# Twelve more paired blocks and a new spreading of the FFT, convolution and weight work in a three-stage token-mixing kernel

## The chip, the cores and the metric

The kernel runs on one core of a Trainium2 chip. The metric is the time of one execution on the device in microseconds, the median of the runs. The core has a matrix engine (PE in the profile; its weight loads are PEld), a vector engine (DVE), a scalar engine (ACT), a general engine (POOL) and a queue that only issues transfers (SP). Each of them works through its own list in order; an instruction waits for semaphores that others raise. Matmuls write to PSUM, which has eight banks here; DVE or ACT read ("evict") the result.

## The reference

Inputs are `x` (4 batches, 4224 tokens, 192 channels) and weights. Three functions follow one another:

```python
def _attn_ref(x, weight):            # 8 heads of 24 channels, 7 taps
    w = softmax(weight, axis=-1)
    x_pad = np.concatenate([np.zeros((B, 6, D)), x], axis=1)
    ...
    out = np.einsum('hk,bskhg->bshg', w, x_unf)
def _moe_ref(x, U, V, w_ch1, w_ch2): # U: 4224x32, V: 32x4224, w_ch1: 192x768, w_ch2: 768x192
    h = x.transpose(0, 2, 1) @ U @ V
    u = x + h.transpose(0, 2, 1)
    return u + np.maximum(u @ w_ch1, 0.0) @ w_ch2
def _moe2_ref(x, w_ch1, w_ch2):
    mixed = np.real(np.fft.fft(np.fft.fft(x, axis=1), axis=2))
    u = x + mixed
    un = (u - mean(u)) / np.sqrt(var(u) + 1e-06)
    return u + np.maximum(un @ w_ch1, 0.0) @ w_ch2
```

## The kernel before

**Blocks.** Tokens are handled in blocks of 384 (three tiles of 128). There are 11 blocks per batch and stage, so 88: stage one is `_moe_ref`'s feed-forward part on the convolved tokens, stage two that of `_moe2_ref` after FFT and normalisation. The list `order` sets which batch and stage come when; blocks 0 to 32 are stage one of batches 0 to 2, 33 to 43 stage two of batch 0, 44 to 54 stage one of batch 3, 55 to 87 stage two of batches 1 to 3.

**Two layers.** Numbers are split into a high and a low 16-bit half. `layer1` makes six `unit`s per block (hidden channels in six groups of 128); each accumulates five matmuls of 384 columns in one PSUM bank: four at L663 and one at L653, `last`. Then `evict` writes `hh` on ACT (L648) and, from it and the bank, `hl` on DVE (L649). `layer2` makes three units of 18 matmuls of 192 columns (L696, L698, L700), which read `hh` and `hl` of all six groups; DVE adds the result to the tokens `u` (L706), and SP stores them (`x2d` at L718 after stage one, `out_d` at L722 at the end). In loop step `i` the first layer of block `i` is mixed with the second layer of block `i - 1`.

**Paired blocks.** The second half of the input channels fills 64 rows only. In a block listed in `PAIRED`, `split_high` also makes a copy of it on the other 64 rows (ACT L580, POOL memset L581; 12 transposed pieces instead of 9), so that `last` runs on 64 rows and two neighbours use different halves of the array. All six units come first then, then the six `last`, then the six evictions.

**Preparation.** While block `i` runs, block `i + 2` is prepared: in stage one, adding `h` (L533, L537, or L525 and L528), `sizes` (L543), `scales` (L548, L551), `high` (L555, L578) and `low` (L562); in stage two `stats` (L596, L598), `root` (L603), `normal` (L608 to L617), `high` (L623, L578) and `low` (L629). `low` runs on POOL, or on DVE in the blocks of `LOWV`, and is followed by the transpose `ch<-sp` on SP (L585). `SLOTS` gives each piece its place among twelve in a step.

**Extra work.** The first units are played from the table `START`. The rest stands in `windows`, lists of units that are spread evenly from step `a` to step `z`, three steps per block: loading and decoding the second stage's weights, the convolutions of batches 2 and 3 (`cv` at L399), and for each batch the two halves of the FFT: gathering rows (`xm`, L758), folding them on DVE and POOL (L792 to L797), splitting (L804 to L806), matmuls `s33` (L825), and then `sd`, `s128` and additions (L865 to L915).

The loop over a block's three thirds sets the order on all engines: two units, slots, `play`, one second-layer unit, `fill`.

Of the kernel before, what the change touches and what calls it, by code (L numbers as in the profile page):

```python
# [32 lines left out]
TB = 3  # L33
# [10 lines left out]
SLOTS = [(5, 5, 7, 7, 9, 10), (0, 4, 4, 9, 9)]  # L44
PAIRED = [(5, 11), (22, 34), (76, 88)]
WARM = 52
AGAIN = (18, 44)
# [51 lines left out]
def build(tc, io):  # L99
# [25 lines left out]
    def run(units):  # L125
        for f in units:
            if f is not None:
                f()

    with tc.manual_schedule():  # L130
# [505 lines left out]
        def layer1(s, b, j):  # L636
# [10 lines left out]
            def evict(m):  # L647
                nc.scalar.activation(hh[:, m], acc[m], AF.Relu)  # L648
                nc.vector.scalar_tensor_tensor(out=hl[:, m], in0=acc[m], scalar=0.0,  # L649
                                               in1=hh[:, m], op0=ALU.max, op1=ALU.subtract)  # L650
# [18 lines left out]
            def pairs():  # L669
                for m in range(NM):  # L670
                    last(m, *((slice(64, P), 2, 3) if m % 2 else (slice(0, 64), 1, 1)))
                for m in range(NM):
                    evict(m)

            if kt == 4:
                return [lambda: run([lambda m=m: unit(m) for m in range(NM)] + [pairs])] + \
                    [lambda: None] * (NM - 1)
            return [lambda m=m: unit(m) for m in range(NM)]
# [284 lines left out]
        part(0)  # L963
        load_uv("u", 0, UH)
# [14 lines left out]

        busy(WARM)  # L980

        def over_taps(a):
            return a.unsqueeze(2).broadcast_to([1, H, KW])

        nc.vector.tensor_reduce(out=wmx, in_=wsm, axis=AX.X, op=ALU.max)
        nc.vector.tensor_tensor(out=wsm, in0=wsm, in1=over_taps(wmx), op=ALU.subtract)
        nc.scalar.activation(wsm, wsm, AF.Exp)
        nc.vector.tensor_reduce(out=wmx, in_=wsm, axis=AX.X, op=ALU.add)
        nc.vector.tensor_scalar(out=wmx, in0=wmx, scalar1=1e-9, scalar2=None, op0=ALU.add)
        nc.vector.reciprocal(wmx, wmx)  # L990
        nc.vector.tensor_tensor(out=row[:, :, ::-1], in0=wsm,
                                in1=over_taps(wmx), op=ALU.mult)
        nc.sync.dma_start(rowd[:, nz:KC * H], rowt[:, nz:])

        load_x(0, 0)
        for i in range(2):
            nc.sync.dma_start(tap[KC * i:KC * i + KC].rearrange("p o h -> p (o h)"), bass.AP(
                tensor=rowd.tensor, offset=rowd.offset, ap=[[H, KC], [1, KC * H]]))
# [14 lines left out]
        jobs = dict(v0=lambda: dec_v(0, 2), B0=lambda: busy(AGAIN[0]), B1=lambda: busy(AGAIN[1]), S=lambda: nc.sync.dma_start(sel, io["sel"]),  # L1013
# [8 lines left out]
        def play(t):  # L1022
            for q in START[t].split() if t < len(START) else ():
                if q in jobs:
                    jobs[q]()
                else:
                    if q[0] in "ab" and q[0] not in queues:
                        queues[q[0]] = [f for _, f in ahead("ab".index(q[0]))]
                    for _ in range(int(q[1:] or 1)):
                        f = queues[q[0]].pop(0)  # L1030
                        if f is not None:
                            f()

        START = [
# [7 lines left out]
        windows = [[28, 32, [load_tables]],  # L1042
                   [15, 60, weights_units(1)],
                   [25, 57, [lambda: load_x(2, 0, 0), lambda: load_x(2, 0, 1), None] + conv_units(2)],
                   [37, 70, ft[0][0]], [70, 100, ft[0][1]],
                   [98, 127, ft[1][0]], [125, 153, ft[1][1]],
                   [65, 120, [lambda: load_x(3, 0, 0), lambda: load_x(3, 0, 1), None] + conv_units(3)],
                   [150, 177, ft[2][0]], [179, 197, ft[2][1]],
                   [190, 215, ft[3][0]], [219, 237, ft[3][1]]]
# [9 lines left out]
        last, pre = None, []  # L1059
        for i in range(nblk + 1):  # L1060
            l1 = layer1(*blocks[i]) if i < nblk else [lambda: None] * NM
            pre = [(n - 12, f) for n, f in pre if n >= 12] + ahead(i + 2)

            def at(n):
                run(f for m, f in pre if m == n)

            soon = any(n < nblk and in_pairs(*blocks[n]) for n in (i + 1, i + 2))
            for r in range(TB):
                l1[2 * r]()
                at(4 * r)  # L1070
                l1[2 * r + 1]()
                at(4 * r + 1)
                play(TB * i + r + 1)
                if i == 1:
                    run(last if r == TB - 1 else [])
                elif last:
                    last[r]()
                at(4 * r + 2)
                fill(TB * i + r)
                at(4 * r + 3)  # L1080
            if soon:
                run(f for n, f in pre if n >= 12)
                pre = []
            ahead_load(i + 4)
            last = layer2(*blocks[i]) if i < nblk else None
# [58 lines left out]
```

## Time and profile before

| | |
|---|---|
| median of 3 runs | 993.72 us (991.71 to 994.56) |
| the profiled execution | 1001.54 us, span of its instructions 999.7 us |
| PE busy | 972.6 us, 97% of the span |
| DVE, ACT, POOL busy | 684.3, 593.8, 380.9 us |
| matmuls | 9929 |

PE is busy nearly all the time, so its list of matmuls and its waits decide. A matmul's own duration is longer than its distance to the next one, since they are pipelined; distances between starts, and whole blocks cut out of the timeline, tell what one costs.

### The profile page before, as it was taken

The page shows a single profiled execution, that of the slowest core. Times are in us where ns is not written, and L with a number is a line of the kernel's source. Part 1 is how long each engine was busy: PE and PEld are TensorE (multiplying, and loading weights), DVE is VectorE, ACT ScalarE, POOL GpSimd, SP SyncE. Part 2 cuts the span into 40 slices and gives each one's busy share as a digit, 9 for nine tenths or more (in the row PEclk, how much of TensorE's full clock was granted, in tenths as well). Part 3 has the DMA queues.
Part 4 walks back from the last instruction along what each step waited for, and adds up shares of the span by engine and source line. Part 5 has one row for each costly group of instructions (what it writes and reads, how often), then busy time and mean ns, then how long its engine had stood idle before and what let it go on. Part 6 is the DMA issues. An engine that isn't in the chain of part 4 may idle for free.

```text
span 999.7 us, 25272 instructions
## 1 busy us (share of the span) xinstructions
PE 972.6 (97%) x9929; PEld 761.5 (76%) x9929; DVE 684.3 (68%) x1918; ACT 593.8 (59%) x1336; POOL 380.9 (38%) x398
## 2 busy tenths in 40 slices
PE   8799999999999999999999999999999999999998
PEld 5477767778777787777878888777887887777776
DVE  7775675569775555567776776777777787666663
ACT  2466456655765666657656566666566675556552
POOL 0111011434642334256533545663266751562110
PEclk9999999999999999999999999999999999999999
DMA  8597975755536665354344545432543432542332
GB/s 293 156 251 227 258 180 156 221 169 153 160 98 192 208 200 147 81 140 122 85 111 125 151 139 148 107 93 67 121 114 95 105 98 65 136 110 56 85 84 64
DMA packets 190655, 139.24 MB, mean 139 GB/s; under 512 B 128170, under 2 KB 164113, under 8 KB 189769
## 3 DMA queue, kind: packets, MB, share of 16 engines
q1 hardware_dynamic: 182951, 124.59, 45.8%
q0 software_dynamic: 7104, 12.70, 4.7%
q8 instruction: 77, 1.26, 0.5%
q14 instruction: 41, 0.34, 0.1%
q10 hardware_dynamic: 482, 0.35, 0.1%
HBM read 61.69 MB, written 46.11 MB: 108 GB/s over the span
## 4 chain that ended last, share of the span: by engine, by line
PE 73%; DVE 8%; DMA 7%; issue 5%; POOL 3%; ACT 3%; SPq 0%; DVEq 0%; POOLq 0%; ACTq 0%
PE l L663 27%; PE l L696 11%; PE l L700 10%; PE l L698 10%; PE l L653 6%; PE cv L399 2%; DMA xm<-x2d,mrow 2%; DMA x1d<-xw 2%; PE sd L865 2%; DVE hl L649 2%; PE s L881 2%; POOL xm L758 2%; PE s L825 1%; DVE x L792 1%; DMA ch<-sp 1%
## 5 line engine op out<-in xcount | busy, mean ns | idle before, releaser
L663 PE MATMUL l<-ch,w1h 128*128 128x384 f16 x1584 | 406.3, 327 | 6.7 <-DMA ch<-sp 2.7
L698 PE MATMUL l<-w2l,hh 128*128 128x192 f16 x1584 | 389.5, 246 | 2.4 <-issue 2.3
L700 PE MATMUL l<-w2h,hl 128*128 128x192 f16 x1584 | 389.6, 246 | 1.8 <-DVE hl L649 1.3
L696 PE MATMUL l<-w2h,hh 128*128 128x192 f16 x1584 | 390.1, 246 | 1.1 <-DVE hl L649 0.5
L649 DVE SCALAR_TENSOR_TENSOR hl<-l,hh 128x384 f16<-128x384 f32 x528 | 270.4, 548 | 155.7 <-ACT hh L648 143.0
L648 ACT ACTIVATE hh<-l 128x384 f16<-128x384 f32 x528 | 233.2, 493 | 124.9 <-PE l L653 117.7
L663 PEld LDWEIGHTS <-w1h 128*128 128x128 f16 x1584 | 155.0, 98 | 95.1 <-issue 4.9
L696 PEld LDWEIGHTS <-hh 128*128 128x128 f16 x1584 | 154.7, 98 | 24.1 <-issue 14.0
L663 PE MATMUL l<-ch,w1l 128*128 128x384 f16 x528 | 172.3, 326 | 0.4 <-issue 0.4
L698 PEld LDWEIGHTS <-hh 128*128 128x128 f16 x1584 | 155.0, 98 | 11.0 <-issue 1.8
L700 PEld LDWEIGHTS <-hl 128*128 128x128 f16 x1584 | 154.9, 98 | 4.3 <-DVE hl L649 2.3
L562 POOL TENSOR_TENSOR sp<-un,sp 128x576 f16<-128x576 f32 x44 | 57.4, 1306 | 249.7 <-ACT sp L578 207.3
L653 PE MATMUL l<-ch,w1l 128*128 128x384 f16 (+1 forms) x528 | 133.7, 327 | 0.0
L758 POOL DMA_INDIRECT xm<-x2d,mrow x84 | 84.6, 1007 | 21.3 <-issue 18.1
L629 POOL TENSOR_TENSOR sp<-un,sp 128x576 f16<-128x576 f32 x34 | 44.1, 1296 | 116.8 <-ACT sp L578 107.2
L623 ACT ACTIVATE un<-u,mr,rs 128x192 f32<-128x192 f32 x132 | 62.4, 537 | 19.6 <-DVE mr L617 19.0
L663 PEld LDWEIGHTS <-w1l 128*128 128x128 f16 x528 | 51.8, 98 | 28.6 <-issue 4.9
L851 POOL DMA_INDIRECT u<-x2d,mrow x64 | 62.2, 972 | 15.3 <-issue 11.4
L653 PEld LDWEIGHTS <-w1l 128*128 128x128 f16 (+1 forms) x528 | 40.4, 97 | 34.2 <-issue 9.9
L578 ACT ACTIVATE sp<-un 128x576 f16<-128x576 f32 x88 | 60.1, 683 | 3.1 <-DMA ch<-sp 0.4
L543 ACT ACTIVATE junk<-u 128x576 f16<-128x576 f32 x44 | 30.0, 681 | 44.2 <-issue 20.0
L706 DVE SCALAR_TENSOR_TENSOR u<-l,ws,u 128x384 f32<-128x384 f32 x88 | 44.2, 510 | 13.8 <-PE l L700 7.8
(137 smaller groups left out, 1135.8 us busy)
## 6 DMA issues: line engine op xcount, KB each, us to landing
x2d<-u SPq DMA_DIRECT2D x68, 288.0 KB
u<-x1d SPq DMA_DIRECT2D x44, 288.0 KB
out_d<-u SPq DMA_DIRECT2D x43, 288.0 KB
x1d<-xw SPq DMA_DIRECT2D x36, 210.0 KB
u<-x2d SPq DMA_DIRECT2D x32, 192.0 KB
x<-x2d SPq DMA_DIRECT2D x60, 99.0 KB
xw<-x_d SPq DMA_DIRECT2D x4, 1344.0 KB
xw<-x_d SPq DMA_DIRECT2D x8, 672.0 KB
```

What stands on the lines that cost most here:

```text
L562: low_engine(0, b, j).tensor_tensor(out=sp[:, :, D:2 * D], in0=k["un"], in1=sp[:, :, :D], op=ALU.subtract)
L578: nc.scalar.activation(sp[:, :, :D], k["un"], AF.Identity)
L623: nc.scalar.activation(un[:, t], u[:, t], AF.Identity, scale=k["r"][:, t:t + 1], bias=k["m"][:, t:t + 1])
L648: nc.scalar.activation(hh[:, m], acc[m], AF.Relu)
L649: nc.vector.scalar_tensor_tensor(out=hl[:, m], in0=acc[m], scalar=0.0, in1=hh[:, m], op0=ALU.max, op1=ALU.subtract)
L653: nc.tensor.matmul(acc[m].rearrange("p (r n) -> p r n", r=TB), lhsT=w["l1"][rows, n, m * P:(m + 1) * P], rhs=kd[x][rows], start=False, sto ...
L663: nc.tensor.matmul(o, lhsT=w[v][:, e, ms], rhs=kd[x], start=(n == 0), stop=False)
L696: nc.tensor.matmul(o, lhsT=hh[:, m, rs], rhs=w["h2"][:, m], start=(m == 0), stop=False)
L698: nc.tensor.matmul(o, lhsT=hh[:, m, rs], rhs=w["l2"][:, m], start=False, stop=False)
L700: nc.tensor.matmul(o, lhsT=hl[:, m, rs], rhs=w["h2"][:, m], start=False, stop=(m == NM - 1))
L758: nc.gpsimd.indirect_dma_start(out=xs[c][1][:, g], out_offset=None, in_=x2d[b][:], in_offset=bass.IndirectOffsetOnAxis(ap=mrow[:99, k:k + ...
L851: nc.gpsimd.indirect_dma_start(out=u2[:, s0 + 2 * e], out_offset=None, in_=src[:], in_offset=bass.IndirectOffsetOnAxis(ap=mrow[:, k2 + e - ...
```

## The change

Forty-two blocks are paired instead of thirty: 4, 11, 12, 20, 21, 34 and 70 to 75 are new. The loop body is replaced by two strings, one for unpaired and one for paired blocks, in which `u` is a unit of the first layer, `l` one of the second layer of the block before, `e` an eviction of a paired block, `a` the next slot of preparation, `p` a step of `START`, `f` a step of the windows. The six evictions of a paired block stand in two groups, five (with a slot between the third and fourth) and one. `SLOTS` and `windows` have other numbers, and the first jobs, before the loop, are named in `START` in the order in which they stood.

```diff
-SLOTS = [(5, 5, 7, 7, 9, 10), (0, 4, 4, 9, 9)]
-PAIRED = [(5, 11), (22, 34), (76, 88)]
+SLOTS = [(3, 4, 7, 7, 9, 10), (0, 4, 4, 9, 10)]
+SEQ = ["uualapfaauauaplafauauaplafa", "uuuauuueeeaeeplafpaaalaeaafaplafa"]
+PAIRED = [(4, 13), (20, 35), (70, 88)]
...
             def pairs():
                 for m in range(NM):
                     last(m, *((slice(64, P), 2, 3) if m % 2 else (slice(0, 64), 1, 1)))
-                for m in range(NM):
-                    evict(m)
-
+
+            units = [lambda m=m: unit(m) for m in range(NM)]
             if kt == 4:
-                return [lambda: run([lambda m=m: unit(m) for m in range(NM)] + [pairs])] + \
-                    [lambda: None] * (NM - 1)
-            return [lambda m=m: unit(m) for m in range(NM)]
+                units[-1] = lambda: (unit(NM - 1), pairs())
+                return units, [lambda m=m: evict(m) for m in range(NM)]
+            return units, []
...
-        windows = [[28, 32, [load_tables]],
-                   [15, 60, weights_units(1)],
-                   [25, 57, [lambda: load_x(2, 0, 0), lambda: load_x(2, 0, 1), None] + conv_units(2)],
+        windows = [[31, 34, [load_tables]],
+                   [9, 58, weights_units(1)],
+                   [28, 57, [lambda: load_x(2, 0, 0), lambda: load_x(2, 0, 1), None] + conv_units(2)],
                    [37, 70, ft[0][0]], [70, 100, ft[0][1]],
-                   [98, 127, ft[1][0]], [125, 153, ft[1][1]],
-                   [65, 120, [lambda: load_x(3, 0, 0), lambda: load_x(3, 0, 1), None] + conv_units(3)],
-                   [150, 177, ft[2][0]], [179, 197, ft[2][1]],
-                   [190, 215, ft[3][0]], [219, 237, ft[3][1]]]
+                   [98, 127, ft[1][0]], [129, 157, ft[1][1]],
+                   [62, 130, [lambda: load_x(3, 0, 0), lambda: load_x(3, 0, 1), None] + conv_units(3)],
+                   [144, 177, ft[2][0]], [179, 197, ft[2][1]],
+                   [190, 215, ft[3][0]], [219, 239, ft[3][1]]]
...
-            for r in range(TB):
-                l1[2 * r]()
-                at(4 * r)
-                l1[2 * r + 1]()
-                at(4 * r + 1)
-                play(TB * i + r + 1)
...
-                at(4 * r + 2)
-                fill(TB * i + r)
-                at(4 * r + 3)
+            for q in SEQ[bool(evicts)]:
+                if q == "u" and l1:
+                    l1.pop(0)()
+                elif q == "e":
+                    evicts.pop(0)()
+                elif q == "l" and last:
+                    last.pop(0)()
+                elif q == "a":
+                    run(f for m, f in pre if m == slot)
+                    slot += 1
...
```

**On PE, in block 20.** Before, the second layer of block 19 follows on the second unit of block 20 (`l1_4093` and `l1_4101` are the banks of units 0 and 1, `l2_4110` that of the second layer):

```order
L663 MATMUL l1_4101<-ch_3901,w1h0_92 128x384
L653 LDWEIGHTS w1l0_93
L653 MATMUL l1_4101<-ch_3901,w1l0_93 128x384
L696 LDWEIGHTS hh_3927
L696 MATMUL l2_4110<-w2h0_94,hh_3927 128x192
```

Now it follows on the six paired matmuls of all six units; line numbers of the changed kernel are one or two lower (`l1_4118`, `l1_4123` and `l1_4128` are the banks of units 3 to 5):

```order
L652 MATMUL l1_4118<-ch_3912,w1l0_93 128x384
L652 LDWEIGHTS w1l0_93
L652 MATMUL l1_4123<-ch_3912,w1l0_93 128x384
L652 LDWEIGHTS w1l0_93
L652 MATMUL l1_4128<-ch_3912,w1l0_93 128x384
L694 LDWEIGHTS hh_3937
L694 MATMUL l2_4150<-w2h0_94,hh_3937 128x192
```

So the second layer of block 19, which needs the evictions of block 19, moved back by four units.

**On DVE, in block 81, near the end, where no extra work stands.** Before, the evictions of block 81 (`l1_14602` and `l1_14607` are its units 4 and 5) come first, and the statistics for block 83 after them:

```order
L649 SCALAR_TENSOR_TENSOR hl_14581<-l1_14602,hh_14580 128x384
L649 SCALAR_TENSOR_TENSOR hl_14581<-l1_14607,hh_14580 128x384
L596 BN_STATS st_14630<-u2_13258 128x6 x3
L598 BN_AGGR mv_14631<-st_14630 128x2 x3
L608 RECIPROCAL rs_14659<-sd_14657 128x3
```

Now the statistics come first, then the evictions of units 0 to 4:

```order
L595 BN_STATS st_14621<-u2_13310 128x6 x3
L597 BN_AGGR mv_14622<-st_14621 128x2 x3
L648 SCALAR_TENSOR_TENSOR hl_14605<-l1_14606,hh_14604 128x384
L648 SCALAR_TENSOR_TENSOR hl_14605<-l1_14611,hh_14604 128x384
L648 SCALAR_TENSOR_TENSOR hl_14605<-l1_14616,hh_14604 128x384
L648 SCALAR_TENSOR_TENSOR hl_14605<-l1_14629,hh_14604 128x384
L648 SCALAR_TENSOR_TENSOR hl_14605<-l1_14634,hh_14604 128x384
L607 RECIPROCAL rs_14681<-sd_14679 128x3
```

The statistics moved in front of the evictions, and the eviction of unit 5 moved behind `normal` and the addition of a second-layer result (L704 in the changed kernel).

## Rows read from the trace of the kernel before

**Rows 1.** The page: busy time, share of the span and instructions of each engine.
```profile
PE 972.6 (97%) x9929; PEld 761.5 (76%) x9929; DVE 684.3 (68%) x1918; ACT 593.8 (59%) x1336; POOL 380.9 (38%) x398
```

**Rows 2.** PE's waits: for whom, us in total, times, longest.
```profile
PE l L663 <- DMA ch<-sp: 2.7, 2, 2.2
PE l L663 <- DVE hl L649: 2.5, 1, 2.5
PE s L825 <- POOL xp L806: 2.3, 3, 1.4
...
PE am L122 <- DVE gm L337: 1.1, 1, 1.1
```

**Rows 3.** Timeline, block 20: start, us, engine, line, instruction, [idle before].
```profile
275.35 0.33 PE L663 MATMUL l<-ch,w1h 128*128 128x384 f16 x1
...
276.19 1.19 DVE L792 TENSOR_TENSOR x<-x,xm 99x760 f32<-99x760 f32 x1 [1.92 <-DMA xm<-x2d,mrow]
...
279.32 0.26 PE L700 MATMUL l<-w2h,hl 128*128 128x192 f16 x1 [1.03 <-DVE hl L649]
```

**Rows 4.** Timeline, block 9, DVE and PE.
```profile
153.19 0.25 DVE L173 TENSOR_SCALAR dec<-u 128x192 int32<-128x192 int32 x1
...
155.12 1.01 DVE L649 SCALAR_TENSOR_TENSOR hl<-l,hh 128x384 f16<-128x384 f32 x2
...
155.72 0.24 PE L533 MATMUL h<-gst,vst 96*128 96x192 f16 x1 [1.76 <-DVE hl L649]
```

**Rows 5.** Timeline of PE, end of block 56.
```profile
675.95 0.67 PE L825 MATMUL s<-vt,xp 99*97 99x102 f16 x10 [1.43 <-POOL xp L806]
```

**Rows 6.** Windows of blocks 70, 72, 80, 81: length, busy us, clock, DMA share, GB/s.
```profile
core 0: us, PE busy (x) PEld busy (x) DVE busy (x) ACT busy (x) POOL busy (x), PEclk, DMA share, GB/s
...
815.01:825.15 10.14, 10.14 (x106) 8.19 (x104) 9.97 (x29) 7.78 (x18) 3.10 (x3) 1.00 0.24 61
834.74:844.07 9.33, 9.33 (x87) 7.39 (x85) 6.39 (x20) 5.01 (x13) 0.00 (x0) 1.00 0.25 65
919.00:928.06 9.06, 9.06 (x87) 6.94 (x86) 5.55 (x19) 5.07 (x13) 1.58 (x3) 1.00 0.31 76
928.06:937.11 9.05, 9.05 (x86) 6.93 (x85) 5.55 (x19) 5.05 (x13) 1.53 (x2) 1.00 0.32 79
```

**Rows 7.** Timeline of PE, end of the first layer of paired block 28.
```profile
366.73 0.49 PE L663 MATMUL l<-ch,w1h 128*128 128x384 f16 x2
367.15 0.66 PE L653 MATMUL l<-ch,w1l 64*128 64x384 f16 x6
367.74 0.26 PE L696 MATMUL l<-w2h,hh 128*128 128x192 f16 x1
```

**Rows 8.** Groups by line and shape: count, busy us, mean ns, idle before.
```profile
L653 PE MATMUL l<-ch,w1l 128*128 128x384 f16 x348 | 113.8, 327 | 0.0
...
L653 PE MATMUL l<-ch,w1l 64*128 64x384 f16 x180 | 19.8, 326 | 0.0
...
L580 ACT ACTIVATE sp<-un 128x192 f16<-128x192 f32 x30 | 10.4, 346 | 0.0
```

**Rows 9.** Timeline of the tail, SP, POOL and PE; block 82 starts at 937.11.
```profile
932.85 1.38 SPq L585 DMA_TRANSPOSE ch<-sp  x1
...
934.33 0.87 SPq L722 DMA_DIRECT2D out_d<-u  x1
...
936.63 0.26 POOL L581 MEMSET sp<- 128x192 f16 x1 [3.81 <-DMA ch<-sp]
...
937.11 0.33 PE L663 MATMUL l<-ch,w1h 128*128 128x384 f16 x1
```

**Rows 10.** Two windows of 4 us, columns as in rows 6.
```profile
82.00:86.00 4.00, 4.00 (x46) 2.98 (x45) 3.11 (x10) 3.26 (x7) 0.89 (x1) 1.00 0.04 15
...
102.00:106.00 4.00, 3.95 (x58) 2.96 (x60) 3.21 (x7) 3.09 (x8) 0.00 (x0) 1.00 1.09 143
```

**Rows 11.** Timeline, SP and PE; block 38 starts at 474.92.
```profile
470.18 1.26 SPq L585 DMA_TRANSPOSE ch<-sp  x1
...
474.92 0.33 PE L663 MATMUL l<-ch,w1h 128*128 128x384 f16 x1
```

More of the change, by code (lines that the diff above doesn't have):

```diff
@@ L42 @@
 PIECE = 5
-SLOTS = [(5, 5, 7, 7, 9, 10), (0, 4, 4, 9, 9)]
-PAIRED = [(5, 11), (22, 34), (76, 88)]
-WARM = 52
-AGAIN = (18, 44)
+SLOTS = [(3, 4, 7, 7, 9, 10), (0, 4, 4, 9, 10)]
+SEQ = ["uualapfaauauaplafauauaplafa", "uuuauuueeeaeeplafpaaalaeaafaplafa"]
+PAIRED = [(4, 13), (20, 35), (70, 88)]
 W_MIN, W_MAX = (float(np.array(w, np.uint32).view(np.float32)) for w in (0x38000000, 0x47EFFFFF))
@@ L962, in build @@
         part = w0_st["st"]["part"]
-        part(0)
-        load_uv("u", 0, UH)
         zer = wrk.tile([1, KC * H], F32, name="hl", tag="hl")
@@ L978, in busy, with soft, taps @@
                                  start=True, stop=True)
-        busy(WARM)
         def over_taps(a):
             return a.unsqueeze(2).broadcast_to([1, H, KW])
[L985 to L998, printed above, removed]
+        def soft():
+            nc.vector.tensor_reduce(out=wmx, in_=wsm, axis=AX.X, op=ALU.max)
+            nc.vector.tensor_tensor(out=wsm, in0=wsm, in1=over_taps(wmx), op=ALU.subtract)
+            nc.scalar.activation(wsm, wsm, AF.Exp)
+            nc.vector.tensor_reduce(out=wmx, in_=wsm, axis=AX.X, op=ALU.add)
+            nc.vector.tensor_scalar(out=wmx, in0=wmx, scalar1=1e-9, scalar2=None, op0=ALU.add)
+            nc.vector.reciprocal(wmx, wmx)
+            nc.vector.tensor_tensor(out=row[:, :, ::-1], in0=wsm,
+                                    in1=over_taps(wmx), op=ALU.mult)
+            nc.sync.dma_start(rowd[:, nz:KC * H], rowt[:, nz:])
+        def taps():
+            for i in range(2):
+                nc.sync.dma_start(tap[KC * i:KC * i + KC].rearrange("p o h -> p (o h)"), bass.AP(
+                    tensor=rowd.tensor, offset=rowd.offset, ap=[[H, KC], [1, KC * H]]))
         uf = ut.rearrange("p n r -> p (n r)")
@@ L1012, in build @@
                       z=[lambda n=n: dec_v(n, n + 1) for n in range(2, 6)])
-        jobs = dict(v0=lambda: dec_v(0, 2), B0=lambda: busy(AGAIN[0]), B1=lambda: busy(AGAIN[1]), S=lambda: nc.sync.dma_start(sel, io["sel"]),
+        jobs = dict(v0=lambda: dec_v(0, 2), M=soft, T=taps, U0=lambda: load_uv("u", 0, UH), S=lambda: nc.sync.dma_start(sel, io["sel"]),
                     V=lambda: load_uv("v", 0, TB * P), V12=lambda: load_uv("v", TB * P, 3 * TB * P),
@@ L1025, in play @@
                     jobs[q]()
+                elif q[0] == "B":
+                    busy(int(q[1:]))
                 else:
@@ L1057, in fill @@
                     done[n] = upto
-        last, pre = None, []
+        last, pre = [], []
         for i in range(nblk + 1):
-            l1 = layer1(*blocks[i]) if i < nblk else [lambda: None] * NM
+            l1, evicts = layer1(*blocks[i]) if i < nblk else ([], [])
             pre = [(n - 12, f) for n, f in pre if n >= 12] + ahead(i + 2)
-            def at(n):
-                run(f for m, f in pre if m == n)
             soon = any(n < nblk and in_pairs(*blocks[n]) for n in (i + 1, i + 2))
-            for r in range(TB):
-                l1[2 * r]()
-                at(4 * r)
-                l1[2 * r + 1]()
-                at(4 * r + 1)
-                play(TB * i + r + 1)
[L1074 to L1077, printed above, removed]
-                at(4 * r + 2)
-                fill(TB * i + r)
-                at(4 * r + 3)
+            slot = steps = fills = 0
+            if i == 1:
+                last = [lambda: None] * 2 + [lambda q=last: run(q)]
+            for q in SEQ[bool(evicts)]:
[8 more added lines that the diff above has]
+                    slot += 1
+                elif q == "p":
+                    play(TB * i + steps + 1)
+                    steps += 1
+                elif q == "f":
+                    fill(TB * i + fills)
+                    fills += 1
             if soon:
@@ L1084, in build @@
             ahead_load(i + 4)
-            last = layer2(*blocks[i]) if i < nblk else None
+            last = layer2(*blocks[i]) if i < nblk else []
         assert all(d == len(w[2]) for d, w in zip(done, windows))
```

2 rows, old and new, of the table START are left out of this document.

## The prediction

> **What bounds the kernel now.** I read the page first. PE is busy for 972.6 of the 999.7 us span, DVE for 684.3, ACT for 593.8, POOL for 380.9 [rows 1], so the end is set by PE's queue, and a change is worth what it takes from PE's matmuls or from the places where PE stands. The list of PE's waits comes next: the longest entries are only 2.7, 2.5, 2.3 and 1.1 us in total [rows 2]. The 2.5 and most of the 2.7 (a single wait of 2.2) fall in front of and inside block 0, where the change alters little. The timeline, cut at the first L663 matmul of each block, shows three of the later ones. In block 20 (first matmul at 275.35) PE had done units 0 and 1 and was inside the second layer of block 19; it stood 1.03 us for `hl` of block 19, because on DVE that eviction stood behind L792, which had itself waited 1.92 us for gathered rows [rows 3]. In block 9 PE stood 1.76 us in L533, for a PSUM bank that `hl` had to free; DVE had first decoded a piece of weights from 153.19 to 155.12 [rows 4]. At the end of block 56 PE stood 1.43 us for POOL's L806, a step of the FFT work [rows 5]. So PE's long waits after block 0 come to 2.3 (all L825) + 1.76 + 1.03 + 1.1 (an `am` matmul, for DVE) = 6.2 us.
>
> How long a block is without extra work is seen where no window has units: block 72, unpaired, is 9.33 us; blocks 80 and 81, paired, are 9.06 and 9.05, PE busy from end to end in all three [rows 6].
>
> **The change, part by part.**
>
> *Twelve more paired blocks* (4, 11, 12, 20, 21, 34, 70 to 75). A paired block runs its six last first-layer matmuls on 64 rows each, two at a time. It is 9.33 - 9.055 = 0.28 us shorter [rows 6]. The joint of a paired block says where the rest of the halving goes: the last two full-height matmuls take 0.42 us from start to start (366.73 to 367.15) and the six half-height ones 0.59 (367.15 to 367.74) [rows 7]. A full-height one costs 9.33 / 57 = 0.164 us (30 of 384 columns and 54 of half that), so the eight would take 1.31 and take 1.01: 0.30, the same saving. That is in line with the busy times of the two forms, 113.8 us for 348 full-height and 19.8 for 180 half-height ones, though a single one lasts as long (327 and 326 ns) [rows 8]. I take 0.28: 12 x 0.28 = **-3.4 us**. The Trainium skill, TensorEngine Tiling (Array Packing), Theoretical Speedup, gives up to twofold for two row tiles; by that the six would cost three slots and the saving would be an estimated 0.49 each, 5.9 us in all, and the sum below would end at 985.5. The same page, Key Properties, says that changing the tiling mode drains the array, and the longer joint above agrees with that.
>
> What pairing adds does not lie on PE: one more ACT copy of 346 ns (L580) per block [rows 8], a POOL memset, and a transpose of twelve pieces rather than nine. ACT is idle for 40% of the span [rows 1]; if that cover were gone, twelve copies would cost 12 x 0.35 = 4.2 us.
>
> *Cover for late evictions.* The PE rows of block 20 show the second move. In an unpaired block the second layer of the block before follows after two units, ten matmuls or 1.6 us; in a paired one after all six, 24 x 0.164 + 0.59 = 4.5 us. The 1.03 us wait [rows 3] is shorter than the 2.9 us that this adds, so it goes: **-1.0 us**. What is late next: the same `hl` is needed 2.9 us later, and behind it DVE has five evictions whose users come a whole block later.
>
> *Two groups of evictions, preparation in front.* In a paired block DVE used to do six evictions and then the statistics for the block after next. Now statistics (or, in stage one, nothing) come first, five evictions, then preparation, then the sixth behind one L706. PE needs the sixth only in the next block's second layer, over 4 us later, so I cost it at nothing; if it were the limit, a late sixth eviction costs one L649 (0.55 us) per paired block at most, 23 us over 42. What it buys is slack: in the tail the transpose for block 82 starts at 932.85, POOL sees it land at 936.63 and PE starts on it at 937.11, 0.5 us to spare [rows 9]. No time is lost there now, so nothing is gained either.
>
> *Weights of stage two loaded and decoded earlier* (window from step 9 rather than 15). The load of 2.3 MB moves from about 105 us, where the DMA engines are full (share 1.09), to about 78 us, ahead of a stretch with a share of 0.04 [rows 10]; decoding then is over before block 9, whose 1.93 us between 153.19 and 155.12 stood in front of its evictions [rows 4]. The ACT eviction before them was itself late, so I take a third: **-0.6 us** (bounds 0 and -1.76).
>
> *FFT windows.* The first half of batch 2 gets steps 144 to 177 instead of 150 to 177, 33 steps for the same 17 units; its `s33` matmuls, twice per block in blocks 53 to 57, come three times in two blocks. That should end the waits for L806 there: of the 2.3 us of L825 I take **-1.5** (bounds 0 and -2.3). The other windows move work between blocks in which PE is full before and after: nothing.
>
> *What twelve more paired blocks can add in waits.* Paired blocks hold six PSUM banks until their evictions; block 9's wait is of this kind, the one long one in 30. Spread over 12 blocks: 1.76 x 12 / 30 = **+0.7** (bounds 0 and, with one like it in every second block, +10).
>
> *Start and end.* The starting part has the same rows on every engine up to block 0, and the last block is paired in both: nothing.
>
> Sum: -3.4 - 1.0 - 0.6 - 1.5 + 0.7 = -5.8 us. The profiled execution took 1001.5 us (span 999.7 and 1.8 around it), 7.8 above the median of 993.7; the terms are differences within PE's queue, so I take them off the median: 987.9, say **988**.
>
> **Rivals.**
>
> *A. Only the matmuls shrink* (chance 0.22). The waits change place and keep their sum: 993.7 - 3.4 = 990.3. For it: nothing removes L792's wait for its gathered rows, it is only hidden. Against: the waits of blocks 20 and 56 [rows 3, 5] stand in blocks whose order changes in the right direction.
>
> *B. Nearly all waits go* (0.15): -3.4 and the whole 6.2 us: 984.1.
>
> *C. The evictions become the bound* (0.14). PE's part of a paired block shrinks, DVE's does not. In block 70, now paired, DVE is busy for 9.97 of 10.14 us [rows 6]; with 0.28 taken off PE it lacks 0.11. If the twelve blocks all were so, none would shorten, and the waits would be no fewer: about 993.5. Against it: in block 72 DVE has 6.39 of 9.33. The Trainium skill, TensorEngine Tiling (Array Packing), PSUM Bottleneck, warns of this: tiling speeds up TensorE but not the emptying of PSUM. By that rule none of the pairing would show.
>
> *D. Slower: the transpose comes too late in stage two* (0.07). Slot 9 became 10 for `low`, so it and its transpose now stand behind the third second-layer unit: 18 short matmuls, 9 x 0.164 = 1.5 us, and on SP behind the `out_d` store, whose issue takes 0.87 us [rows 9]: up to 2.3 us later. In block 38 the transpose started at 470.18 for a use at 474.92, 4.74 us [rows 11]; one takes at most 936.63 - 932.85 = 3.8 [rows 9]. The spare is 0.9, so such a block would lose 1.4 us. It decides from five such blocks among stage two's unpaired ones (with the 5.8 gained); with six it ends near 996, with seven near 998. Against it: in block 38 POOL was late for other reasons, which hold the slot's place anyway, and in the paired tail the statistics start 3 us earlier than the transpose is put back.
>
> **How the numbers follow.** Forecast 0.42 (985 to 990.5), A 0.22, B 0.15, C 0.14, D 0.07. No change means within 0.3%, 990.7 to 996.7, about what a measurement of this kernel can tell. Faster: the forecast, B, and half of A, whose 990.3 lies at the bound: 0.68. Same: the other half of A, C, and a third of D: 0.27. Slower: 0.05. The range goes from 983, 1 us under B, to 993.5, C's time, and leaves out D and the tails of B and C, under 0.2. A and C end on the side of no gain, so the likeliest case has its own range, 985 to 990.5.
>
> **What would show it.** In the profile after: PE busy down by 3 to 4 us and the half-height L653 matmuls 252 instead of 180; blocks 72 to 75 shorter by 0.28 for the same extra work; no wait of PE for `hl` in the second layer in block 20; none for L806 in blocks 53 to 57; in the tail 1 us or more between the landing of the transpose and its use. I am wrong if PE's waits for `ch` add up to more than 3 us (D), if DVE is full over several paired blocks and PE waits for `hl` there (C), or if the weights' load at 78 us delays a `ch` or `u` of blocks 4 to 6.

## The result and the profile after

The changed kernel takes 983.48 us (median of 5 runs, 983.06 to 984.84) against 992.34 us of the kernel before in the same comparison (5 runs, 991.71 to 994.56): ratio 0.9909, interval 0.9896 to 0.9922. It is 8.9 us faster. The forecast was 5.8 us (988). The stated range, 983 to 993.5, just holds the time; the range of the likeliest case, 985 to 990.5, does not; and rival B (984.1) was nearer than the forecast.

The page of the profiled execution after (span 981.3 us), beside [rows 1]:

```profile
PE 964.2 (98%) x9929; PEld 755.6 (77%) x9929; DVE 688.2 (70%) x1918; ACT 595.7 (61%) x1348; POOL 388.4 (40%) x410
```

The same 9929 matmuls keep PE busy for 8.4 us less. About 3 us of that belong to the one execution that was profiled before: in a second profile of that kernel (before_look, below) the same 9162 matmuls from block 4 on keep PE busy for 893.8 us instead of 896.9. PE's longest waits after, beside [rows 2] (for whom, us in total, times, longest; line numbers are one or two lower than before):

```profile
PE l L662 <- DVE rc L550: 2.2, 1, 2.2
PE l L662 <- DVE hl L648: 1.8, 1, 1.8
...
PE am L121 <- DVE gm L336: 1.1, 1, 1.1
...
PE s L823 <- POOL xp L804: 1.0, 2, 0.5
...
PE s L823 <- DVE z L831: 0.7, 1, 0.7
```

The first two stand in front of and inside block 0, as before. The waits for `xp` fell from 2.3 to 1.0 (what is left stands in blocks 19 and 20), those for `hl` in the second layer and in L533 (now L532) have left the list, and one for DVE's `z` is new, in block 19. The timeline after, beside [rows 3, 4]: first block 9 (DVE and PE), then block 20 (PE):

```profile
151.47 2.42 DVE L648 SCALAR_TENSOR_TENSOR hl<-l,hh 128x384 f16<-128x384 f32 x5 [1.42 <-ACT hh L647]
...
152.66 0.41 PE L532 MATMUL h<-gst,vst 96*128 96x192 f16 x3
...
273.48 0.32 PE L662 MATMUL l<-ch,w1h 128*128 128x384 f16 x1 [0.34 <-DVE cmax L547]
...
274.91 0.66 PE L652 MATMUL l<-ch,w1l 64*128 64x384 f16 x6
275.50 0.26 PE L694 MATMUL l<-w2h,hh 128*128 128x192 f16 x1
...
281.53 0.67 PE L823 MATMUL s<-vt,xp 99*97 99x102 f16 x10 [0.50 <-POOL xp L804]
```

In block 9 the evictions run without a decoding in front of them and PE does not stand in L532. In block 20 the second layer (from 275.50) runs without a wait for `hl`, but PE now waits inside the units for `cmax`, and for `xp` at the block's end. Windows of blocks 70, 72 and 80 after, columns as in [rows 6]:

```profile
800.44:810.31 9.87, 9.87 (x106) 7.75 (x104) 9.61 (x28) 7.15 (x18) 3.29 (x4) 1.00 0.29 71
819.62:828.67 9.05, 9.05 (x86) 6.93 (x85) 6.82 (x22) 5.53 (x14) 0.26 (x1) 1.00 0.32 78
...
901.02:910.08 9.06, 9.06 (x88) 6.94 (x85) 6.98 (x23) 5.54 (x14) 1.53 (x2) 1.00 0.32 78
```

Blocks 70 and 72, newly paired, are 0.27 and 0.28 us shorter (10.14 to 9.87 and 9.33 to 9.05). Block 70 did so with DVE at 9.61 of 9.87 us. The groups of the last first-layer matmul, beside [rows 8], and the tail, beside [rows 9], where block 82 now starts at 919.13:

```profile
L652 PE MATMUL l<-ch,w1l 128*128 128x384 f16 x276 | 90.0, 326 | 0.0
L652 PE MATMUL l<-ch,w1l 64*128 64x384 f16 x252 | 27.8, 326 | 0.0
```

```profile
912.95 1.45 SPq L584 DMA_TRANSPOSE ch<-sp  x1
...
916.72 0.26 POOL L580 MEMSET sp<- 128x192 f16 x1 [3.79 <-DMA ch<-sp]
```

The transpose has landed 2.4 us before its use; before, it was 0.5.

### The profile page after: what moved, and what is told of

It reads as the page before. It is cut to its first block, busy times and chain, and to the rows that moved or that the text cites. A ratio compares the mean times of both kernels' runs of the same rounds, so it can differ in the third digit from the quotient of the medians.

```text
span 981.3 us, 25290 instructions
## 1 busy us (share of the span) xinstructions
PE 964.2 (98%) x9929; PEld 755.6 (77%) x9929; DVE 688.2 (70%) x1918; ACT 595.7 (61%) x1348; POOL 388.4 (40%) x410
## 4 chain that ended last, share of the span: by engine, by line
PE 90%; DMA 4%; DVE 2%; ACT 1%; issue 1%; POOL 1%; SPq 0%; ACTq 0%; DVEq 0%; POOLq 0%
PE l L662 34%; PE l L694 13%; PE l L698 13%; PE l L696 13%; PE l L652 7%; PE s L823 2%; PE cv L398 2%; PE sd L863 2%; PE s L879 2%; DMA x1d<-xw 1%; PE gp L414 1%; PE h L532 1%; DMA u<-wc_d 1%; DMA ch<-sp 1%; DMA tap<-rowd 1%
## 5 line engine op out<-in xcount | busy, mean ns | idle before, releaser
L662 PE MATMUL l<-ch,w1h 128*128 128x384 f16 x1584 | 395.4, 326 | 5.2 <-DVE rc L550 2.2
L698 PE MATMUL l<-w2h,hl 128*128 128x192 f16 x1584 | 389.6, 246 | 0.0
L698 PEld LDWEIGHTS <-hl 128*128 128x128 f16 x1584 | 154.9, 98 | 1.2 <-issue 1.1
L561 POOL TENSOR_TENSOR sp<-un,sp 128x576 f16<-128x576 f32 x44 | 59.3, 1348 | 203.8 <-ACT sp L577 174.2
L652 PE MATMUL l<-ch,w1l 128*128 128x384 f16 (+1 forms) x528 | 117.8, 326 | 0.0
L628 POOL TENSOR_TENSOR sp<-un,sp 128x576 f16<-128x576 f32 x34 | 45.2, 1330 | 84.6 <-ACT sp L577 80.9
L652 PEld LDWEIGHTS <-w1l 128*128 128x128 f16 (+1 forms) x528 | 35.8, 96 | 33.9 <-issue 13.3
L704 DVE SCALAR_TENSOR_TENSOR u<-l,cmax,u 128x384 f32<-128x384 f32 x88 | 44.9, 511 | 14.2 <-PE l L698 13.6
```

The lines of the kernel that those rows point to most:

```text
L561: low_engine(0, b, j).tensor_tensor(out=sp[:, :, D:2 * D], in0=k["un"], in1=sp[:, :, :D], op=ALU.subtract)
L652: nc.tensor.matmul(acc[m].rearrange("p (r n) -> p r n", r=TB), lhsT=w["l1"][rows, n, m * P:(m + 1) * P], rhs=kd[x][rows], start=False, sto ...
L662: nc.tensor.matmul(o, lhsT=w[v][:, e, ms], rhs=kd[x], start=(n == 0), stop=False)
L698: nc.tensor.matmul(o, lhsT=hl[:, m, rs], rhs=w["h2"][:, m], start=False, stop=(m == NM - 1))
```

## The experiments

All kernels are the changed one with constants put back or varied. Three parts can be exchanged: the list of pairs (P), the order inside a block (O: the two strings and `SLOTS`), and the windows (W). The old order, written as strings:

```diff
-SLOTS = [(3, 4, 7, 7, 9, 10), (0, 4, 4, 9, 10)]
-SEQ = ["uualapfaauauaplafauauaplafa", "uuuauuueeeaeeplafpaaalaeaafaplafa"]
+SLOTS = [(5, 5, 7, 7, 9, 10), (0, 4, 4, 9, 9)]
+SEQ = ["uauaplafauauaplafauauaplafa", "uuuuuueeeeeeaaplafaaaplafaaaplafa"]
```

The runs of one group below shared one chip, each group another, and every ratio is against the kernel before on that chip.

| group | kernel | P O W | median us | ratio, interval |
|---|---|---|---|---|
| 1 | before | | 1002.37 | |
| 1 | pairs_only | new old old | 1003.9 | 1.0015, 0.9999 to 1.0032 |
| 1 | order_only | old new old | 1001.63 | 0.9997, 0.998 to 1.0014 |
| 1 | windows_only | old old new | 998.8 | 0.9966, 0.9949 to 0.9982 |
| 2 | before | | 993.05 | |
| 2 | after_again | new new new | 983.31 | 0.991, 0.9883 to 0.9937 |
| 2 | no_pairs | old new new | 987.16 | 0.9944, 0.9927 to 0.9961 |
| 2 | no_order | new old new | 987.88 | 0.9943, 0.9923 to 0.9963 |
| 2 | no_windows | new new old | 990.47 | 0.9981, 0.9962 to 1.0 |
| 3 | before | | 1001.68 | |
| 3 | weights_late | new new, weights old | 996.84 | 0.9945, 0.9928 to 0.9961 |
| 3 | fft_old | new new, FFT old | 997.72 | 0.9961, 0.9944 to 0.9977 |
| 3 | windows_only_2 | old old new | 999.1 | 0.9977, 0.9961 to 0.9992 |
| 3 | pairs_only_2 | new old old | 1003.27 | 1.002, 1.0003 to 1.0038 |
| 4 | before | | 994.06 | |
| 4 | whole_third | new new new | 983.82 | 0.9896, 0.9874 to 0.9917 |
| 4 | pairs_only_3 | new old old | 991.84 | 0.9977, 0.9961 to 0.9993 |
| 4 | prep_behind | one string other | 987.88 | 0.9932, 0.9908 to 0.9955 |
| 4 | all_paired | 84 pairs | 991.24 | 0.9978, 0.9961 to 0.9995 |
| 5 | before | | 994.16 | |
| 5 | thirteen_more | 55 pairs | 979.41 | 0.9855, 0.9829 to 0.9881 |

**Each part alone** (group 1). Theory 1: the parts add up, as the terms of the prediction do. Theory 2, its rival: pairing pays only with the new order. With it the kernel before was profiled once more, for PE's waits without a releaser ("issue" in the list of waits: time in which PE waited for nothing that the profile shows). In the first profile of before they came to 5.5 us from block 4 on.

> Only the list of paired blocks is new (42); order within a block, slots and windows as before. Theory 1, the parts add up: PE's matmuls shrink by 12 x 0.28 = 3.4 us and the waits of PE stay, so 989 us beside 992.3 for the kernel before, with block 72 at 9.05 us. Theory 2, pairing pays only with the new order of evictions and preparation: in the twelve new blocks PE waits take back 2 us or more, 991 us or above.

> Only the order within a block and the slots are new (evictions in two groups, preparation in front); 30 paired blocks, windows as before. Theory 1: PE's waits inside the old paired blocks (6, 8, 9, 26, 76, 86, together 4.7 us in the profile before) shrink by 1 to 3 us, the others stay: 989.5 to 991.5. Theory 2: the order has no gain of its own, 992 +-1, since it only makes room for more pairs.

> Only the windows of extra work are new. Theory 1: the waits of blocks 53 to 56 for the FFT's splitting go (2.8 us) and so does the 1.9 us in block 9, behind the decoding of weights: 988 us, 4 us less than before. Theory 2: the windows only fit the shorter blocks; waits move elsewhere, 991 to 993.

> The kernel before, profiled a second time. Its first profile spans 999.7 us though its runs have a median of 992.3, and holds about 7.6 us in which PE waits for nothing that the profile shows (blocks 14, 33, 42, 64, 73). Theory 1: these belong to that one execution; the second profile lacks them and spans about 991 us, with the same waits for hl, xp and gm at the same blocks. Theory 2: they belong to the kernel, and stand at the same blocks again.

On this chip only the windows gave something measurable. The second profile of before took 1005.34 us and showed the waits without a releaser again. Theory 1 had expected 3.4 us less for the pairs; that fell. In order_only the wait that rival D described does stand in one place, in front of block 38:

```profile
473.00 0.34 PE L662 MATMUL l<-ch,w1h 128*128 128x384 f16 x1 [1.29 <-DMA ch<-sp]
```

On SP the transpose now follows the `out_d` store, as D said. No profile of before has this wait; so the order by itself made one there. But the chip was another one, so the whole change had to be measured beside its parts.

**One part left out** (group 2).

> The whole change, on the same chip as the runs with one part left out. Additive theory: the three parts alone gave 1.0015 (pairs), 0.9997 (order) and 0.9966 (windows) of the kernel before, so that together they give 0.998. Interaction theory: the 0.991 of the first measurement comes back, and 0.7% of it belongs to parts only in company. If it is 0.991, the three runs beside it, each with one part taken out, say which company.

> Order and windows new, the 30 old paired blocks. If pairing pays its 0.28 us a block once the new order is there, this stands 3 to 4 us above the whole change (0.9945 of before). If the pairs bring nothing even then (as pairs alone did), it stands within 1 us of it (0.991 to 0.992). Additive theory: 0.9963.

> 42 paired blocks and new windows, with the old order inside a block (six units, six evictions, preparation behind them). If the new order is what makes pairs pay, 12 more pairs here bring nothing over windows alone: 0.996 to 0.998 of before, 5 to 7 us above the whole change. If windows are what makes pairs pay, 0.992 to 0.993. Additive theory: 0.998.

> 42 paired blocks and the new order, old windows. If the new order makes pairs pay, 0.9955 to 0.9965 of before (3.4 us of matmul time, less than the whole change by the windows' 3.4 us). If only the windows make pairs pay, 1.000 as the order alone and the pairs alone. Additive theory: 1.001.

The whole change keeps its 0.991. Leaving out the pairs costs 3.9 us, the order 4.6, the windows 7.2. These sum to 15.6, more than the 9.7 of the whole (993.05 - 983.31): each part's worth includes waits that only the other parts make or leave room for. The profiles from block 4 on say the same: 3.0, 3.2 and 6.2 us more than after_again. In no_windows PE stands for `hl` again in block 9 (1.58) and for `xp` in blocks 55 and 56 (0.60 and 1.43), but also in block 6 (1.1; 0.5 in the first profile of before, none in the later before_look) and in front of block 38 (0.53, for `ch`; none in any profile of before). So with the old windows the new order and pairs make waits of their own. With windows and pairs together (no_order) the ratio is lower than with windows alone in group 1, but that is another chip; whether pairs pay with the old order is shown by pairs_only_3 below. In the profile of no_pairs, block 20 (unpaired there) has its old wait back:

```profile
274.29 0.26 PE L698 MATMUL l<-w2h,hl 128*128 128x192 f16 x1 [0.87 <-DVE hl L648]
```

Yet that block takes 11.96 us in no_pairs and 11.66 after: 0.30, the pairing's own 0.28 and nothing for the cover.

**Two windows put back, two parts alone again** (group 3).

```diff
-                   [9, 58, weights_units(1)],
+                   [15, 60, weights_units(1)],
```

> The whole change with only the weights' window put back to start at step 15. Theory W: the decoding in front of block 9's evictions was worth the whole of its wait: 1.8 to 2.0 us above the whole change (0.993 of before), with the wait of about 1.75 us of L533 (or what stands there) back in block 9 or next to it. The prediction's term: 0.6 us above. If early weights matter in more places (the transfers of the weights against the transposes of blocks 1 to 6), more than 2.5 us.

```diff
-                   [98, 127, ft[1][0]], [129, 157, ft[1][1]],
+                   [98, 127, ft[1][0]], [125, 153, ft[1][1]],
...
-                   [144, 177, ft[2][0]], [179, 197, ft[2][1]],
-                   [190, 215, ft[3][0]], [219, 239, ft[3][1]]]
+                   [150, 177, ft[2][0]], [179, 197, ft[2][1]],
+                   [190, 215, ft[3][0]], [219, 237, ft[3][1]]]
```

> The whole change with only the three FFT windows put back (second halves of batches 1 and 3, first half of batch 2). Theory F: the waits of the s matmuls for POOL's xp in blocks 53 to 57 come back, 2.3 to 2.8 us above the whole change (0.9935 of before). The prediction's term: 1.5 us above. If the windows' worth of 7 us in company lies mostly here: 4 us or more.

> The windows alone once more, where the PE time without a releaser (7 us in the profiles of before, pairs alone, order alone and windows alone, none in the whole change and in the three kernels with one part left out) may be absent. Theory chip: this idle time belongs to the chip or the execution; where it is absent the windows alone give 5 to 7 us (0.993 to 0.995) and the parts add up nearly. Theory company: windows alone give 0.9966 again.

> The twelve further pairs alone once more. Theory chip: 0.9965 (3.4 us of matmuls less). Theory company: 1.000 to 1.002 again, with the data waits of PE in blocks 20, 33, 34, 55, 73 and 76 that took the saving the first time.

weights_late: the decoding is back in front of block 9's evictions, and PE stands in L532 again:

```profile
153.24 0.25 DVE L172 TENSOR_SCALAR dec<-u 128x192 int32<-128x192 int32 x1
...
155.18 2.41 DVE L648 SCALAR_TENSOR_TENSOR hl<-l,hh 128x384 f16<-128x384 f32 x5
...
155.78 0.24 PE L532 MATMUL h<-gst,vst 96*128 96x192 f16 x1 [1.59 <-DVE hl L648]
```

A second wait, 0.75 us for DVE's L122, stands in block 6 at 114.52. fft_old: the waits for `xp` in blocks 53 to 57 are back, the longest of them as before [rows 5], and in block 73 PE stands for `rp`:

```profile
673.83 0.57 PE L823 MATMUL s<-vt,xp 99*97 99x102 f16 x8 [1.43 <-POOL xp L804]
...
850.21 0.20 PE L879 MATMUL s<-rp,vt 128*128 128x97 f16 x1 [1.22 <-ACT rp L868]
```

The whole change was not run on this chip. Against its 0.99 elsewhere, the two ratios put the weights' window at about 4 us and the FFT windows at 5 to 6 us. PE's data waits that are back, and that the whole change does not have, come to 2.7 us in blocks 6 and 9 for the weights, and to 4.4 us for the FFT, 2.6 of them in blocks 53 to 56 and the rest in blocks 73 and 76. The parts alone gave here about what they gave in group 1.

**The pairs alone on a chip like that of group 2, the order's core, and all pairs** (group 4).

> The whole change on whichever chip this is. If the gain belongs to the kernel: 0.991 of before again, also where PE's waits without a releaser are there. If it came only where those are absent, and a chip that has them takes part of it: 0.994 to 0.997.

> The twelve further pairs alone. On a chip with PE's waits without a releaser: 1.002 again. On a chip without them: 0.9965 if only those waits ate the saving; 1.000 if the data waits in blocks 73 and 76 and the late transposes of the tail do.

```diff
-"uuuauuueeeaeeplafpaaalaeaafaplafa"
+"uuuuuueeeeeeaaplafpaaalaaafaplafa"
```

> The whole change with the string of a paired block changed alone: six units, six evictions, then the preparation. The prediction's price for two groups and preparation in front: nothing, so within 1 us of the whole change. If this is what the new order is worth: 3 to 5 us above it, with waits for ch or sd in blocks 82 to 86 and for rp in block 73, as the kernel with the old order showed.

```diff
-PAIRED = [(4, 13), (20, 35), (70, 88)]
+PAIRED = [(4, 88)]
```

> Blocks 4 to 87 all paired, 42 more than in the whole change. If the term of 0.28 us holds in every block: 11.8 us less than the whole change. If late second layers and held banks cost where DVE, ACT and POOL carry FFT work (rival C): less than half of it, or slower, with PE waiting for hl or u in blocks 13 to 19 and 35 to 69.

pairs_only_3 gains 2.2 us of the 3.4; in groups 1 and 3 the same kernel gained nothing. So pairs can pay with the old order, and theory 2 in its strict form falls as well. They also make waits. before_look and pairs_only_3, both without the waits that lack a releaser, differ by the twelve pairs alone; PE at the same place in block 73, first without and then with them:

```profile
843.02 0.43 PE L881 MATMUL s<-rp,vt 128*128 128x97 f16 x6
```

```profile
844.92 0.38 PE L879 MATMUL s<-rp,vt 128*128 128x97 f16 x5 [1.02 <-DVE rp L869]
```

From block 4 on, PE is busy for 2.9 us less in pairs_only_3 and idle for 2.6 us more. prep_behind is 4.1 us slower than the whole change (medians of six runs each, with ranges that do not overlap). Its profile shows one place clearly, block 73 (DVE and PE):

```profile
838.06 1.01 DVE L648 SCALAR_TENSOR_TENSOR hl<-l,hh 128x384 f16<-128x384 f32 x2
...
838.99 0.87 DVE L595 BATCH_NORM_STATS2 st<-u 128x6 f32<-128x192 f32 x3
...
841.84 0.35 DVE L869 TENSOR_TENSOR rp<-sd,rp 128x194 f16<-128x194 f32 x1
...
842.24 0.38 PE L879 MATMUL s<-rp,vt 128*128 128x97 f16 x5 [1.36 <-DVE rp L869]
```

Statistics and their small followers stand between the evictions and the product of the FFT (L869) that PE needs. After the whole change the statistics are done before the evictions, and L869 comes in time:

```profile
829.21 0.87 DVE L595 BATCH_NORM_STATS2 st<-u 128x6 f32<-128x192 f32 x3
...
837.75 0.35 DVE L869 TENSOR_TENSOR rp<-sd,rp 128x194 f16<-128x194 f32 x1
838.00 0.54 PE L879 MATMUL s<-rp,vt 128*128 128x97 f16 x6
```

all_paired is 7.4 us slower than the whole change, although 42 blocks more are paired. PE's waits there:

```profile
PE l L662 <- DMA ch<-sp: 9.6, 6, 2.2
PE s L823 <- POOL xp L804: 4.5, 7, 1.2
PE s L823 <- DVE z L831: 2.4, 3, 1.7
```

They stand, blocks 0 and 2 apart, in blocks 14 to 19, 36 to 40, 50 to 54 and 63 to 69. That the evictions, put behind all six units, push back what the transposes and the FFT need is the likely reason, but it was argued from the order and not tested. In most of the other blocks, among them 41 to 49 and 56 to 62, the saving is there (0.15 to 0.28 us) and no wait.

**Thirteen more pairs, and a second profile of before** (group 5).

```diff
-PAIRED = [(4, 13), (20, 35), (70, 88)]
+PAIRED = [(4, 13), (20, 35), (41, 48), (56, 62), (70, 88)]
```

> The whole change with blocks 41 to 47 and 56 to 61 paired as well, thirteen in which all_paired showed the 0.28 us and no wait. If the term holds block by block: 3.6 us less than the whole change, 0.987 of before. If pairing only pays or fails by the neighbourhood (the block before or after being paired too): waits for ch, u or hl at the edges (blocks 48 to 51, 55, 62 to 64) and less than 2 us.

> One profile of the kernel before. If PE's waits without a releaser belong to the chip: none where the runs of before are near 993, and then a span of about 992; 6 to 7.6 us of them, at blocks 14, 33, 42, 64 and 73, where the runs are near 1002. If they belong to the profile: here in either case.

thirteen_more is the fastest kernel of the study: 979.41 us, 1.45% less than before, some 4 us less than the whole change on other chips; from block 4 on its profile is 3.5 us shorter, with 3.6 expected. Its windows of blocks 44 and 58:

```profile
525.57:535.92 10.35, 10.35 (x110) 8.22 (x108) 5.79 (x15) 5.47 (x14) 4.18 (x6) 1.00 0.53 135
671.52:680.83 9.31, 9.31 (x95) 7.19 (x94) 7.24 (x24) 5.33 (x15) 0.26 (x1) 1.00 0.31 77
```

After the whole change these blocks took 10.63 and 9.59: 0.28 each; of the thirteen only block 43 saves less, 0.19. before_look took 992.89 us with a span of 991.1 and has, apart from 0.6 us in front of one matmul, no wait of PE without a releaser. So profiling alone does not make them; they go with the chip, or with the occasion.

## Why the prediction had the direction right and the size too small

**The step that failed** is the price of single parts, each read off the waits of the kernel before. The prediction put "two groups, preparation in front" at nothing; put back alone, it costs 4.1 us. It charged +0.7 for waits that the pairs would add; with the new order next to none came. It took 0.6 us for the earlier weights, a third of the wait of block 9, and the whole wait of 1.76 us went. The size of the pairs' own saving, the largest term, was right.

before_look and whole_third are two profiles without the waits that lack a releaser, so their difference (991.1 to 981.6, 9.5 us) can be split by place. The windows are: start to block 4, blocks 4 to 13, 14 to 21, 22 to 47, 48 to 57, 58 to 69, 70 to 79, 80 to the end. Only the first two columns count here, length and PE busy. First before:

```profile
0.00:86.25 86.25, 75.41 (x770) 52.07 (x771) 61.69 (x165) 39.86 (x91) 8.70 (x15) 0.98 0.78 229
86.25:206.56 120.31, 117.26 (x1292) 88.93 (x1290) 77.72 (x219) 71.21 (x168) 24.40 (x26) 1.00 0.73 203
206.56:296.07 89.51, 87.83 (x907) 69.84 (x904) 68.70 (x176) 60.36 (x130) 44.63 (x41) 1.00 0.59 151
296.07:575.40 279.33, 278.97 (x2920) 221.99 (x2919) 182.08 (x499) 175.96 (x402) 122.07 (x129) 1.00 0.53 143
575.40:681.08 105.68, 103.83 (x1027) 83.88 (x1026) 77.14 (x206) 70.16 (x150) 59.90 (x57) 1.00 0.43 114
681.08:807.47 126.39, 126.39 (x1284) 103.02 (x1283) 100.22 (x291) 79.09 (x170) 70.60 (x70) 1.00 0.45 109
807.47:910.18 102.71, 102.30 (x1025) 81.98 (x1023) 74.41 (x227) 61.21 (x141) 41.61 (x50) 1.00 0.38 95
910.18:991.10 80.92, 77.23 (x728) 59.78 (x726) 43.89 (x139) 37.56 (x90) 10.46 (x13) 1.00 0.30 72
```

And after:

```profile
0.00:85.03 85.03, 77.58 (x771) 53.18 (x772) 61.79 (x165) 40.74 (x92) 9.02 (x17) 0.96 0.81 247
85.03:201.47 116.44, 115.05 (x1259) 86.75 (x1258) 79.46 (x228) 70.97 (x168) 24.27 (x27) 1.00 0.76 202
201.47:292.28 90.81, 88.77 (x938) 70.12 (x935) 67.29 (x166) 61.16 (x132) 45.23 (x41) 1.00 0.58 157
292.28:569.41 277.13, 277.13 (x2902) 220.55 (x2901) 181.49 (x496) 176.12 (x402) 120.25 (x127) 1.00 0.52 140
569.41:674.41 105.00, 104.64 (x1047) 84.85 (x1045) 79.49 (x210) 70.95 (x153) 68.81 (x65) 1.00 0.47 125
674.41:800.80 126.39, 126.39 (x1285) 103.02 (x1284) 101.72 (x292) 79.56 (x172) 67.62 (x70) 1.00 0.46 108
800.80:901.37 100.57, 100.57 (x1024) 79.26 (x1022) 73.60 (x229) 60.06 (x147) 42.68 (x54) 1.00 0.42 102
901.37:981.60 80.23, 77.06 (x729) 59.86 (x726) 44.13 (x137) 36.65 (x89) 10.48 (x13) 1.00 0.28 72
```

Extra work moved between stretches, so lengths alone mislead: blocks 14 to 21 grew by 1.3 us with 31 more matmuls. Summed from block 4 on, PE's busy time fell from 893.82 to 889.60, by 4.2, and its idle time (length less busy) from 11.04 to 6.96, by 4.1. The start gave the other 1.2. The forecast had 3.4 for the matmuls, 2.4 for the waits (3.1 gone less 0.7 added) and nothing for the start. Three profiles of the whole change agree within 0.03 us from block 4 on; of before, only before_look is free of the other waits. Of the idle time, 1.8 us went in block 9, 1.9 in blocks 55 and 56, and 1.3 in blocks 37, 76, 85 and 87, and 0.4 in blocks 14 and 20, while 1.1 came up in blocks 19 and 50.

*Twelve pairs, -3.4: right.* 0.28 us a block in blocks 70 and 72, 3.9 us by the run without them (3.0 from block 4 on in its profile), and 0.28 again in twelve of the thirteen further blocks. The Trainium skill's twofold (TensorEngine Tiling (Array Packing), Theoretical Speedup), which would have made it an estimated 0.49 a block, is not borne out.

*Cover in block 20, -1.0: wrong.* The `hl` wait went as said, but no_pairs shows that the block lost only the pairing's own share; waits for `cmax` and `xp` came up in the same block (0.84 us together, where no_pairs has 0.87 for `hl`). Here the cover gained nothing, since other work was as late.

*Two groups, preparation in front, 0: the term that was furthest off.* prep_behind puts this one point back and loses 4.1 us; 3.1 of them stand from block 4 on in the profiles (899.67 against 896.57 us). The prediction looked for a time that was lost before the change and found none in the tail. By block, 1.8 us of the 3.1 stand in the newly paired blocks 73 and 20. The wait of block 73 is one that the twelve pairs make with the old order: before_look has none there, pairs_only_3 has 1.02 us and prep_behind 1.36. The rest is not of that kind: 0.6 us stands in block 85, paired before as well, where before_look also waits for `ch` (0.20), and 0.5 in block 8. Which of the two, the groups or the preparation in front, does it was not separated. The new string for unpaired blocks and `SLOTS`, for which the prediction had only rival D, are left with the 0.5 us by which the order's 4.6 in group 2 exceeds these 4.1, no more than noise.

*Added waits, +0.7: did not come, for that reason.* It is the same item priced twice, without seeing the link: with the old order the pairs cost waits (1.2 us of their 3.4 by the median of pairs_only_3, all of it in groups 1 and 3), with the new one only those of block 20, which took the place of the old wait.

*Weights earlier, -0.6: too small.* The whole wait of block 9 went, 1.76 [rows 4], the bound that the prediction named and gave a third of. The argument that ACT's eviction was late too missed that decoding had made it late: in the kernel before another piece of it stood on DVE in block 8, in front of the `rc` that ACT waited for.

```profile
144.81 0.25 DVE L173 TENSOR_SCALAR dec<-u 128x192 int32<-128x192 int32 x1
```

Without both pieces five evictions run in a row from 151.47, and PE finds its bank free.

*FFT windows, -1.5: a little too small.* Only two of the three L825 waits stood in blocks 53 to 57 (0.44 and 1.43 us, in blocks 55 and 56; the third, 0.48, in block 19). These two went entirely, and the one of block 19 stayed. By the ratio across chips, putting the windows back costs more than the two did. Whether the wait of block 73 in fft_old is due to the windows or to that chip is open: no_windows, on another chip, has none there.

*The other windows, nothing: not so.* All windows together were priced at 2.1 us. Alone they gave 2.6 and 3.6, and taken out of the whole change they cost 7.2, in part because the new order and pairs make waits in block 6 and in front of block 38 with the old ones. The one of block 6 is back in weights_late; which window removes the other was not tested.

*Start, nothing: the difference here is 1.2.* The start took 84.0 to 85.0 us in three profiles of the whole change and 85.3, 86.3 and 88.1 in three of before. It varies by as much with one kernel, and no run tests it.

*From the median, not from the profile: right.* The profiled execution stood 7.8 us above the median; before_look shows an execution at 992.89 without the waits that lacked a releaser. The reading of [rows 2] did leave these out: they were 2.3 us at L698 and 1.8 at L663, about as long as those that it named.

Rival A (waits only change place) fails by the 4.1 us of idle time, C by block 70. D fails since after the change PE waits for `ch` only in blocks 0 to 2; but order_only and no_windows show its wait in front of block 38 (1.29 and 0.53 us), so D was right of the order with the old windows, in one block of the five that it needed. all_paired shows that what C feared comes in another form, late transposes and late FFT products. It comes among blocks with FFT work, but not in all of them: block 64, where DVE and POOL are busy for 0.96 and 0.69 of the time in whole_third, still saves 0.28 us in all_paired. Rival B's number (984.1) was close partly by luck: it let 6.2 us of waits go, 4.1 of idle time went, and the start and PE's busy time gave the rest.

## What to carry to other kernels

When a change makes one engine's bursts denser and at the same time moves other work in front of them, do not price the two apart: the order is also worth the waits that the denser bursts would make, which do not stand in the profile before. In this kernel a long single wait with an identified cause was worth its whole length when the work that caused it left the place (block 9), and nothing when it was only covered and another wait stood close behind (block 20). Where a local saving holds in some blocks, apply it everywhere once, read block by block where it was eaten, and keep the rest: that gave the best kernel here.

## What the runs showed of the hardware

The same program ran at two speeds, each group on another chip: the runs of before had medians of 993.05, 994.06 and 994.16 us on three occasions and 1002.37 and 1001.68 on two others. The profiles differ in waits of PE in front of which no releaser is shown. Between the first profile of before and before_look 9.5 us differ from block 4 on: 5.5 us are such waits, and 3.1 us a longer busy time for the same matmuls. Block 64, 104 matmuls in either case, took 12.08 us in the first profile of before and 10.37 in before_look:

```profile
750.45:762.53 12.08, 11.11 (x104) 8.16 (x102) 8.01 (x27) 5.05 (x12) 5.60 (x6) 1.00 0.38 89
```

```profile
744.93:755.30 10.37, 10.37 (x104) 8.42 (x102) 10.10 (x31) 5.65 (x14) 7.17 (x7) 1.00 0.52 134
```

They recur in block 64 in fft_old and weights_late too (0.16 to 0.92 us each), which differ from the whole change, profiled on other chips without them, by three lines and by one. Their cause was not found: each chip was used on one occasion only, so chip and occasion are not told apart. The DMA queue that loads instructions took the same share (0.5%) in the first profile of before and in before_look, so a slower loading does not show there. Where they are present the ratios of the parts came out otherwise: pairs alone gave 0.9977 where they are absent and 1.0015 and 1.002 where they are not.
